# Gated linear attention and SwiGLU: scores and state product moved into 32-column groups of the array, causal mask by predicated copy

## The chip, the cores and the metric

The kernel runs on one core of one Trainium2 chip. The metric is device time in microseconds (us) of one execution. TensorE is called PE in the profile, its weight loads PEld, VectorE is DVE, ScalarE is ACT, GpSimd is POOL and SyncE, which here only issues DMAs, is SP.

## The reference

Two blocks follow each other, everything in fp32. The first is a recurrence for each of 4 batches and 8 heads over 768 positions, with head size 48 and one complex decay per position and feature:

```python
for t in range(S):
    ar, ai = (a_re_n[:, :, t, :, None], a_im_n[:, :, t, :, None])
    new_re = ar * S_re - ai * S_im
    new_im = ar * S_im + ai * S_re
    kv = np.einsum('bhd,bhe->bhde', k[:, :, t], v[:, :, t])
    S_re, S_im = (new_re + kv, new_im)
    y[:, :, t] = np.einsum('bhd,bhde->bhe', q[:, :, t], S_re)
```

`a_re_n` and `a_im_n` are the decay with its magnitude capped at 0.999. The second block takes y as 3072 tokens of 384 features, divides each by its root mean square, scales it, and applies a feed-forward layer of width 1536: `silu(x @ w_gate) * (x @ w_val) @ w_out`.

## The kernel before

**Tiling.** The 768 positions of a batch are cut into chunks of 128 (`C`), which makes 24 chunks. Two chunks form a group of the feed-forward (12 groups), and from the third on also a unit of the decay work. The recurrence becomes matrix products inside a chunk and a state carried from chunk to chunk.

**Stages.** `gates(u)` turns the decays of a unit into cumulative magnitudes and phases on ACT and DVE, multiplies q and k by them (tile `rot`), and moves the result with six DMAs per chunk into `kq`: 96 rows (48 features times cosine and sine part), per head 128 columns of k and 128 of q. `attend(n)` then does for chunk n:

- scores: for each head one product of k (96x128, the stationary operand) with q (96x128, streamed), which gives 128 key positions s by 128 query positions t; four heads fill one PSUM bank (banks 4 and 5, variable `a`). DVE multiplies each bank by a 0/1 matrix `causal` into `am` (line 1080);
- the output, transposed (features by positions): 12 blocks of 32 features, each the sum of `ve` (v, with each pair of heads padded to 80 columns per head so that a block of 32 may be cut anywhere) times `am`, and of the previous state times q. Each block goes to one of four groups of 32 columns of the array, chosen by the 32 PSUM partitions that it writes, and the list is ordered so that the four groups take turns;
- where the batch goes on: k is transposed on PE into `kt` (positions by 96), and the state product adds `kt`^T v for each head: stationary 128x96, streamed 48 columns (line 1112);
- the norm: squares on ACT, a column sum on PE, a power on POOL, and a spread of the result over the partitions on PE, then `xT` on DVE.

`feed(g, xT)` is the feed-forward of a group: 144 fp32 products of 256 columns for `w_gate` and `w_val`, then the output product, from group 2 on as seven products of half size (a Strassen-like scheme that uses the sums of `weight_sums`). An fp32 product appears in the trace as two PE records, one for each pass; the transposes appear as one.

**Order of the work.** Nothing is issued in the order of the source. `Flow` records every operation with an estimated duration and the memory it touches (`note` takes a PSUM bank as a whole), `dates` gives each a due time counted back from its users, and `schedule` picks on every engine the ready operation that is due first. `issue` then emits the instructions in that order, so all of them carry line 648 in the profile and are told apart by their tiles. Each engine runs its own instructions strictly in this order. A changed estimate, or one more operation, can move any other operation on any queue. The feed-forward's due times come from a running sum (`clock`), and attention work is placed between its products.

**Names that the change touches.** `causal`, `ams`, `ves`, `states` (buffers, lines 796 to 830), the fills at the start on POOL (`fill`), `attend` (line 1069), and its estimates passed to `mms`. `moved[n]` are the six moves into `kq` of chunk n, behind which the loads of v are held (`behind=`). SP is the queue for all loads and moves but the weights, which POOL issues.

Of the kernel before, what the change touches and what calls it, by code (L numbers as in the profile page):

```python
# [9 lines left out]
I32 = mybir.dt.int32  # L10
# [4 lines left out]
ALU = mybir.AluOpType  # L15
# [4 lines left out]
C = 128  # L20
BLK = 32
# [440 lines left out]
class Flow:  # L462
# [56 lines left out]
    def add(self, eng, calls, dur, reads=(), writes=(), table=None, land=None, due=None, after=(), behind=()):  # L519
        op = dict(i=len(self.ops), eng=eng, calls=calls, dur=dur, deps=set(), table=table, land=land,  # L520
                  base=due, stage=self.stage, behind={o["i"] for o in behind})
        self.ops.append(op)
        op["deps"].update(o["i"] for o in after)
        for ap in reads:
            self.note(op, ap, False)
        for ap in writes:
            self.note(op, ap, True)
        return op
# [122 lines left out]
def fast(tc, ctx, qT, kT, v, a_re, a_im, w_gate, w_val, w_out, rms_g, out, H, bad):  # L651

    nc = tc.nc
    B, DM, S = a_re.shape
    D = DM // H
    D2 = 2 * D
# [22 lines left out]
    def room(name, shape, dtype=FP32):  # L679
        t = mem.tile(shape, dtype, name=name, tag=name)  # L680
        row = 1
        for x in shape[1:]:
            row *= x
        rooms[t.tensor.name] = (name, row * mybir.dt.size(dtype))
        keep.append(t)
        return t
# [25 lines left out]
    def tt(o, x, y, op=ALU.mult, eng="DVE", **kw):  # L712
        e = nc.vector if eng == "DVE" else nc.gpsimd
        dur = 0.15 + 1.04e-3 * cols(o) if eng == "DVE" else 0.25 + 2.2e-3 * cols(o)
        return add(eng, [(e.tensor_tensor, (), dict(out=o, in0=x, in1=y, op=op))], dur, [x, y], [o], **kw)
# [51 lines left out]
    def dma(o, x, eng="SP", **kw):  # L767
        n = mybir.dt.size(o.dtype)
        for s in o.shape:
            n *= s  # L770
        row = mybir.dt.size(o.dtype) * min(run(o), run(x))
        load = n / row * (0.006 + 50.3e-6 * row) / 16
        op = add(eng, [(QUEUE[eng].dma_start, (), dict(out=o, in_=x))], 0.85 if eng == "POOL" else 0.62, [x], [o],
                 land=2.0 + 1.4 * load, **kw)
        op["load"] = load
        op["packet"] = max(0.07, 0.006 + 50.3e-6 * row * (2 if eng == "POOL" and row == 2048 else 1))
        return op

    def mms(list_, dur, **kw):
        calls, reads, writes = [], [], []  # L780
        for o, l, r, start, stop in list_:
            calls.append((nc.tensor.matmul, (o,), dict(lhsT=l, rhs=r, start=start, stop=stop)))
            reads += [l, r]
            writes.append(o)
        return add("PE", calls, dur, reads, writes, **kw)

    def mm_time(n, m=P):
        return 2 * max(0.84e-3 * n, 0.83e-3 * m)
# [4 lines left out]


    ident = room("ident", [P, P])
    causal = room("causal", [C, C])
    mhalf = room("mhalf", [P, 1])
    ones = room("ones", [P, 1])
    halfpi = room("halfpi", [P, 1])
# [24 lines left out]
    ams = [room(f"am{i}", [C, H, C]) for i in range(2)]  # L824
    kts = [room(f"kt{i}", [C, H, D2]) for i in range(1)]
    ves = [room(f"ve{i}", [C, NP, 2, 80]) for i in range(3)]
    states = [room(f"state{i}", [D2, NP, 2, 80]) for i in range(2)]
    sqs = [room(f"sq{i}", [P, ND, C]) for i in range(1)]
    ygs = [room(f"yg{i}", [P, ND, C]) for i in range(2)]
# [16 lines left out]
    for t in ves + states:  # L846
        fill(t[:, :, :, D:], 0.0)
    add("POOL", [(make_identity, (nc, ident), {})], 0.6, [], [ident])
    fill(causal, 1.0)
    add("POOL", [(nc.gpsimd.affine_select, (), dict(out=causal, in_=causal, pattern=[[1, C]],  # L850
                                                    compare_op=ALU.is_ge, fill=0.0, base=0,
                                                    channel_multiplier=-1))], 0.3, [causal], [causal])
    dma(gcol, rms_g.rearrange("(c p) -> p c", p=P))


# [213 lines left out]
    def attend(n):  # L1069
        flow.stage = "attend", n  # L1070
        ve, am, kq = ves[n % 3], ams[n % 2], kqs[n % 2]
        vv = ve[:, :, :, 0:D].rearrange("t m e d -> t (m e) d")
        dma(vv, v[n * C:(n + 1) * C, :].rearrange("t (h d) -> t h d", d=D), behind=moved[min(n - 1, HOLD)] if n else ())
        k, q = kq[:, :, 0:C], kq[:, :, C:2 * C]
        for a in range(2):
            ps = banks[4 + a]
            s = ps.rearrange("s (h t) -> s h t", h=HH)
            mms([(s[:, h], k[:, a * HH + h], q[:, a * HH + h], True, True) for h in range(HH)],
                HH * mm_time(C), due=EARLY.get(n))
            tt(am[:, a * HH:(a + 1) * HH], s, causal.unsqueeze(1).to_broadcast([C, HH, C]))  # L1080
        first, last = n % NCH == 0, n % NCH == NCH - 1
        prev, new = states[(n + 1) % 2], states[n % 2]
        ps = banks[6]
        yT = ps[:, 0:DM].rearrange("p (j t) -> p j t", j=ND)
        lines = [[] for _ in range(4)]
        vf, sf = (x.rearrange("p m e d -> p m (e d)") for x in (ve, prev))
        for i in range(4 * ND):
            j, c = divmod(i, 4)
            m, r = divmod(i, 3)
            o = yT[c * BLK:(c + 1) * BLK, j]  # L1090
            part = [(2 * m, 0)] if r == 0 else [(2 * m, 1), (2 * m + 1, 2)] if r == 1 else [(2 * m + 1, 3)]
            todo = []
            for h, g in part:
                todo.append((vf[:, m, g * BLK:(g + 1) * BLK], am[:, h]))
                if not first:
                    todo.append((sf[:, m, g * BLK:(g + 1) * BLK], q[:, h]))
            for x, (l_, r_) in enumerate(todo):
                lines[c].append((o, l_, r_, x == 0, x == len(todo) - 1))
        order = [lines[c][i] for i in range(len(lines[0])) for c in range(4)]
        mms(order, len(order) * mm_time(C) / 4 * 1.1 + 0.15)  # L1100
        if not last:
            kt = kts[0]
            for a in range(2):
                ps = banks[7 - 3 * a]
                kp = ps[:, 0:HH * D2].rearrange("t (h d) -> t h d", h=HH)
                calls = [(nc.tensor.transpose, (kp[:, h], k[:, a * HH + h], ident[0:D2, 0:D2]), {})
                         for h in range(HH)]
                add("PE", calls, HH * 0.085, [k[:, a * HH:(a + 1) * HH], ident], [kp])
                act(kt[:, a * HH:(a + 1) * HH], kp, AF.Copy)
            ps = banks[5][0:D2, 0:DM]  # L1110
            st = ps.rearrange("p (h d) -> p h d", h=H)
            mms([(st[:, h], kt[:, h], vv[:, h], True, True) for h in range(H)], H * mm_time(D, D2))
            st4 = ps.rearrange("p (m e d) -> p m e d", m=NP, e=2)
            u, i = unit_of[n], n - UNITS[unit_of[n]][0]
            decay = decays[way_of(u)][:, :, i].rearrange("p (m e) -> p m e", e=2).unsqueeze(3).to_broadcast([D2, NP, 2, D])
            new4 = new[:, :, :, 0:D]
            if first:
                tt(new4, st4, decay)
            else:
                tt(new4, st4, prev[:, :, :, 0:D], ALU.add)  # L1120
                tt(new4, new4, decay)

        flow.stage = "norm", n
        sq, yg = sqs[0], ygs[n % 2]
        act(sq, yT, AF.Square)
        if unit_of[n] in LIGHT:
            for j in range(ND):
                act(yg[:, j], yT[:, j], AF.Copy, scale=gcol[:, j:j + 1])
        else:
            tt(yg, yT, gcol.unsqueeze(2).to_broadcast([P, ND, C]))  # L1130
            tt(sq[:, 0], sq[:, 0], sq[:, 1], ALU.add)
            tt(sq[:, 0], sq[:, 0], sq[:, 2], ALU.add)
        ps = banks[7]
        col = ps[:, C:C + 1]
        parts = range(ND if unit_of[n] in LIGHT else 1)
        mms([(col, sq[:, j], ones, j == 0, j == parts[-1]) for j in parts], 0.25 * len(parts))
        sv = ssv[:, n:n + 1]
        ts(sv, col, 1.0 / DM, EPS_RMS, ALU.mult, ALU.add)
        add("POOL", [(nc.gpsimd.tensor_tensor, (), dict(out=rss[n % 2], in0=sv, in1=mhalf,
                                                        op=ALU.pow))], 0.9, [sv, mhalf], [rss[n % 2]])  # L1140
        wide = ps[:, 0:C]
        mms([(wide, rss[n % 2].to_broadcast([P, P]), ident, True, True)], 0.25)
        g = group_of[n]
        ns = GROUPS[g]
        x, lo = xplace[g]
        wide_ = len(ns) * C
        xT = xTs[x][:, lo:lo + ND * wide_].rearrange("p (j t) -> p j t", j=ND)
        i = n - ns[0]
        tt(xT[:, :, i * C:(i + 1) * C], yg, wide.unsqueeze(1).to_broadcast([P, ND, C]))
        return xT  # L1150
# [190 lines left out]
```

## Time and profile before

| | us |
|---|---|
| median of 3 runs | 740.79 (740.71 to 741.93) |
| profiled execution, its own time | 740.29 |
| its span, first to last instruction | 738.6 |
| PE busy in the span | 694.7 (94%) |
| PEld busy | 623.9 (84%) |
| DVE busy | 470.6 (64%) |
| ACT busy | 332.1 (45%) |
| POOL busy | 39.4 (5%) |
| first product of the feed-forward starts at | 55.41 |

The table is read from the top: the span is what the instructions explain, and the profiled execution's own time is 1.7 us longer. Busy shares are averages over a start in which PE waits for the first decays and weights, and a long stretch in which it hardly waits at all. PE's busy time is the union of its records; the records overlap because the array is pipelined, so how long a product holds the array is read from the distance between the starts of records, not from their durations.

### The profile page before, as it was taken

The page shows a single profiled execution, that of the slowest core. Times are in us where ns is not written, and L with a number is a line of the kernel's source. Part 1 is how long each engine was busy: PE and PEld are TensorE (multiplying, and loading weights), DVE is VectorE, ACT ScalarE, POOL GpSimd, SP SyncE. Part 2 cuts the span into 40 slices and gives each one's busy share as a digit, 9 for nine tenths or more (in the row PEclk, how much of TensorE's full clock was granted, in tenths as well). Part 3 has the DMA queues.
Part 4 walks back from the last instruction along what each step waited for, and adds up shares of the span by engine and source line. Part 5 has one row for each costly group of instructions (what it writes and reads, how often), then busy time and mean ns, then how long its engine had stood idle before and what let it go on. Part 6 is the DMA issues. An engine that isn't in the chain of part 4 may idle for free.

```text
span 738.6 us, 12320 instructions
## 1 busy us (share of the span) xinstructions
PE 694.7 (94%) x5050; PEld 623.9 (84%) x5050; DVE 470.6 (64%) x738; ACT 332.1 (45%) x450; POOL 39.4 (5%) x71
## 2 busy tenths in 40 slices
PE   0369999999999999999999999999999999999996
PEld 0368877877899899899899899899899899899885
DVE  5989987779987977967646546656834234233121
ACT  8567656937576925813915623722821110110010
POOL 3132100000000000000000000000000000000000
PEclk9968999999999999999999999999999999999999
DMA  8697565536455355535222202314111102200000
GB/s 298 209 294 235 161 154 166 163 82 169 127 138 149 99 154 150 181 106 146 70 65 66 75 12 73 95 27 119 54 40 30 51 12 55 65 1 2 22 0 27
DMA packets 100144, 76.47 MB, mean 104 GB/s; under 512 B 40944, under 2 KB 90864, under 8 KB 100080
## 3 DMA queue, kind: packets, MB, share of 16 engines
q1 hardware_dynamic: 96016, 61.05, 30.3%
q0 software_dynamic: 3264, 14.16, 5.3%
q8 instruction: 42, 0.69, 0.4%
q10 hardware_dynamic: 800, 0.39, 0.2%
q14 instruction: 22, 0.18, 0.1%
HBM read 51.91 MB, written 4.72 MB: 77 GB/s over the span
## 4 chain that ended last, share of the span: by engine, by line
PE 92%; DVE 4%; ACT 1%; POOL 1%; issue 1%; DMA 1%; DVEq 0%; POOLq 0%; ACTq 0%
PE bank L648 92%; DVE wg L648 1%; DVE turns L648 1%; DVE wv L648 1%; DMA in<-in_a_re_dram 1%; ACT t L648 0%; DVE t L648 0%; DVE rot L648 0%; ACT L648 0%; DVE in L648 0%; POOL rs L648 0%; DVE xT L648 0%; ACT turns L648 0%; DVE am L648 0%; ACT wo L648 0%
## 5 line engine op out<-in xcount | busy, mean ns | idle before, releaser
L648 PE MATMUL bank<-xT,wg 128*128 128x256 f32 x864 | 201.0, 383 | 1.9 <-DVE xT L648 1.9
L648 PE MATMUL bank<-xT,wv 128*128 128x256 f32 x864 | 198.4, 379 | 0.0
L648 PEld LDWEIGHTS bank<-xT,wg 128*128 128x128 f32 x864 | 164.8, 192 | 25.1 <-DVE xT L648 2.6
L648 PEld LDWEIGHTS bank<-xT,wv 128*128 128x128 f32 x864 | 163.5, 190 | 22.2
L648 DVE TENSOR_TENSOR hT<-bank,sg 128x512 f32<-128x512 f32 x72 | 49.6, 689 | 120.9 <-PE bank L648 114.9
L648 PE MATMUL bank<-wo,hT 128*128 128x192 f32 (+1 forms) x576 | 123.4, 357 | 0.4 <-DVE hT L648 0.4
L648 PEld LDWEIGHTS bank<-wo,hT 128*128 128x128 f32 x576 | 94.4, 190 | 11.8 <-issue 1.4
L648 ACT ACTIVATE sg<-bank 128x512 f32<-128x512 f32 x72 | 43.0, 597 | 130.4 <-PE bank L648 127.4
L648 ACT ACT_TABLE_LOAD x67 | 86.0, 1283 | 7.3 <-DVE rot L648 4.7
L648 PE MATMUL bank<-kq 96*128 96x128 f32 x384 | 52.3, 290 | 28.2 <-DMA kq<-rot 28.2
L648 PEld LDWEIGHTS bank<-kq 96*128 96x128 f32 x384 | 49.5, 203 | 29.8 <-issue 29.0
L648 ACT ACTIVATE sq<-bank 128x384 f32<-128x384 f32 x24 | 11.8, 491 | 106.7 <-PE bank L648 106.6
L648 DVE TENSOR_TENSOR rot<-kin,turns 128x768 f32<-128x768 f32 x48 | 44.6, 952 | 14.6 <-DMA kq<-rot 14.4
L648 POOL TENSOR_TENSOR rs<-ssv,mhalf 128x1 f32<-128x1 f32 x24 | 19.4, 810 | 586.6 <-DVE ssv L648 498.0
L648 ACT ACTIVATE kt<-bank 128x384 f32<-128x384 f32 x40 | 18.5, 489 | 66.0 <-PE bank L648 65.9
L648 PE MATMUL bank<-sums,hT 128*128 128x192 f32 x240 | 45.1, 329 | 0.0
L648 PEld LDWEIGHTS bank<-sums,hT 128*128 128x128 f32 x240 | 39.4, 190 | 0.0
L648 DVE TENSOR_TENSOR hT<-hT 128x768 f32<-128x768 f32 x40 | 38.2, 955 | 0.9
L648 PE MATMUL bank<-am,ve 128*32 128x128 f32 x768 | 37.8, 281 | 0.0
L648 ACT ACTIVATE turns<-in 128x768 f32<-128x768 f32 (+1 forms) x39 | 29.9, 789 | 17.1 <-DVE rot L648 8.0
L648 DVE TENSOR_TENSOR am<-bank,causal 128x512 f32<-128x512 f32 x48 | 32.7, 686 | 7.1 <-PE bank L648 6.5
L648 ACT ACTIVATE t<-t 128x768 f32<-128x768 f32 (+1 forms) x39 | 30.9, 792 | 7.9 <-DVE t L648 7.2
(108 smaller groups left out, 729.0 us busy)
## 6 DMA issues: line engine op xcount, KB each, us to landing
kq<-rot SPq DMA_DIRECT2D x144, 128.0 KB, 2.4
ve<-in_v_dram SPq DMA_DIRECT2D x24, 192.0 KB, 3.1
kin<-in_q_dram SPq DMA_DIRECT2D x24, 192.0 KB, 2.7
kin<-in_k_dram SPq DMA_DIRECT2D x24, 192.0 KB, 4.1
wo<-in_w_gate_dram SPq DMA_DIRECT2D x6, 768.0 KB, 5.7
out_dram<-ot SPq DMA_DIRECT2D x24, 192.0 KB, 2.2
wo<-in_w_val_dram SPq DMA_DIRECT2D x6, 768.0 KB, 4.3
wo<-in_w_out_dram SPq DMA_DIRECT2D x6, 768.0 KB, 4.3
```

The lines of the kernel that those rows point to most:

```text
L648: fn(*args, **kw)
```

## The change

- **Scores.** Instead of one product of 128 stationary columns per head, there are four per head, each with one block of 32 key positions as the stationary operand. Block b streams only the query positions from 32b on (128, 96, 64 and 32 columns); what lies left of it is masked anyway. Block b of an even head is written to partitions 32b to 32b+31, that of an odd head to block 3-b, so that two heads together give every column group 160 columns. The estimate becomes 0.29 per pair of heads.
- **Mask.** Because part of each bank is not written, the product with `causal` becomes a predicated copy: `am` is zeroed once at the start, and only positions where the mask is set are copied from PSUM. The mask has two forms, natural and with its four row blocks reversed; `causal` doubles and is made by eight selects. Banks 4 and 5 are zeroed once on DVE.
- **v.** The odd heads' `am` has its row blocks reversed, so `ve` must hold v of the odd heads with row blocks reversed: one DMA for the even heads and four for the odd ones. The state product needs the natural order, so v is read a second time, whole rows, into the new single buffer `vn`.
- **State product.** The 96 stationary columns of a head are cut into three groups of 32: 24 products per chunk instead of 8, each streaming 48 columns. The estimate becomes 0.1 per head.

```diff
-    causal = room("causal", [C, C])
+    causal = room("causal", [C, 2, C])
...
+    vns = [room(f"vn{i}", [C, H, D]) for i in range(1)]
...
     fill(causal, 1.0)
-    add("POOL", [(nc.gpsimd.affine_select, (), dict(out=causal, in_=causal, pattern=[[1, C]],
-                                                    compare_op=ALU.is_ge, fill=0.0, base=0,
-                                                    channel_multiplier=-1))], 0.3, [causal], [causal])
+    for e in range(2):
+        for b in range(4):
+            x = causal[b * BLK:(b + 1) * BLK, e]
+            add("POOL", [(nc.gpsimd.affine_select, (), dict(out=x, in_=x, pattern=[[1, C]],
+                                                            compare_op=ALU.is_ge, fill=0.0,
+                                                            base=-BLK * (3 - b if e else b),
+                                                            channel_multiplier=-1))], 0.3, [x], [x])
+    for t in ams:
+        fill(t, 0.0)
+    for t in banks[4:6]:
+        fill(t, 0.0, eng="DVE")
...
-        vv = ve[:, :, :, 0:D].rearrange("t m e d -> t (m e) d")
-        dma(vv, v[n * C:(n + 1) * C, :].rearrange("t (h d) -> t h d", d=D), behind=moved[min(n - 1, HOLD)] if n else ())
+        first, last = n % NCH == 0, n % NCH == NCH - 1
+        vv = vns[0]
+        later = dict(behind=moved[min(n - 1, HOLD)] if n else ())
+        rows = v[n * C:(n + 1) * C, :].rearrange("t (m e d) -> t m e d", e=2, d=D)
+        dma(ve[:, :, 0, 0:D], rows[:, :, 0], **later)
+        for b in range(4):
+            dma(ve[(3 - b) * BLK:(4 - b) * BLK, :, 1, 0:D], rows[b * BLK:(b + 1) * BLK, :, 1], **later)
+        if not last:
+            dma(vv.rearrange("t h d -> t (h d)"), v[n * C:(n + 1) * C, :], **later)
...
-            mms([(s[:, h], k[:, a * HH + h], q[:, a * HH + h], True, True) for h in range(HH)],
-                HH * mm_time(C), due=EARLY.get(n))
-            tt(am[:, a * HH:(a + 1) * HH], s, causal.unsqueeze(1).to_broadcast([C, HH, C]))
-        first, last = n % NCH == 0, n % NCH == NCH - 1
+            list_ = []
+            for h in range(HH):
+                for b in range(4):
+                    c = 3 - b if h % 2 else b
+                    list_.append((s[c * BLK:(c + 1) * BLK, h, b * BLK:], k[:, a * HH + h, b * BLK:(b + 1) * BLK],
+                                  q[:, a * HH + h, b * BLK:], True, True))
+            mms(list_, HH // 2 * 0.29, due=EARLY.get(n))
+            pairs = lambda t: t.rearrange("s (m e) t -> s m e t", e=2)
+            mask = causal.bitcast(I32).unsqueeze(1).to_broadcast([C, HH // 2, 2, C])
+            o = am[:, a * HH:(a + 1) * HH]
+            add("DVE", [(nc.vector.copy_predicated, (), dict(out=pairs(o), mask=mask, data=pairs(s)))],
+                0.15 + 1.04e-3 * HH * C, [causal, s, o], [o])
...
-            mms([(st[:, h], kt[:, h], vv[:, h], True, True) for h in range(H)], H * mm_time(D, D2))
+            mms([(st[c * BLK:(c + 1) * BLK, h], kt[:, h, c * BLK:(c + 1) * BLK], vv[:, h], True, True)
+                 for h in range(H) for c in range(3)], H * 0.1)
```

In the order of instructions that results, the pieces of attention lie elsewhere between the feed-forward's products, and the start is arranged anew on every queue. PE enters 32-column products in 53 separate stretches after the first product of the feed-forward, against 23 before (22 of them the output of a chunk, and one product for the final check). After that point there are 22 chunks of scores and 18 state products.

## Prediction

> **What bounds the kernel now.** I first read the chain that ended last, in order of time (start us, us, what):
>
> ```profile
> 55.41 58.15 PE bank L648 x386
> ...
> 116.60 0.46 DVE xT L648
> ...
> 117.10 567.96 PE bank L648 x4226
> ...
> 686.15 40.45 PE bank L648 x200
> ```
>
> From 55.41 to the end at 738.6 the chain is PE's own queue but for some 12 us. The stage table (length, busy time and records of each engine, clock, DMA share) says that the others have room there:
>
> ```profile
> 117.10:686.10 569.00, 568.16 (x4228) 515.44 (x4228) 360.91 (x581) 249.98 (x327) 14.43 (x20) 1.00 0.32 88
> ```
>
> PE is busy for 568.2 of 569.0 us, DVE for 361, DMA for 0.32. So what counts is the array time of the touched products, read from starts in PE's timeline (start, us, instruction):
>
> ```profile
> 317.30 1.48 PE L648 MATMUL bank<-ve,kt 128*96 128x48 f32 x16
> 318.62 1.12 PE L648 MATMUL bank<-kq 96*128 96x128 f32 x8
> 319.58 2.75 PE L648 MATMUL bank<-xT,wv 128*128 128x256 f32 x12
> 322.17 1.06 PE L648 MATMUL bank<-kq 96*128 96x128 f32 x8
> 323.07 0.82 PE L648 MATMUL bank<-ident,kq 96*128 96x96 f32 x8
> ```
>
> A state product holds PE for 318.62-317.30 = 1.32 us (16 records of 0.083), half the scores for 323.07-322.17 = 0.90 (8 of 0.112). Then a stretch in 32-column groups, the output of a chunk:
>
> ```profile
> 337.05 1.14 PE L648 MATMUL bank<-sums,hT 128*128 128x192 f32 x6
> 338.12 0.42 PE L648 MATMUL bank<-am,ve 128*32 128x128 f32 x8
> 338.36 0.40 PE L648 MATMUL bank<-kq,state 96*32 96x128 f32 x8
> 338.58 0.40 PE L648 MATMUL bank<-am,ve 128*32 128x128 f32 x8
> ...
> 339.68 0.40 PE L648 MATMUL bank<-kq,state 96*32 96x128 f32 x8
> 340.01 1.24 PE L648 MATMUL bank<-hT 128*128 128x192 f32 x6
> 341.09 0.38 PE L648 MATMUL bank<-ident,rs 128*128 128x128 f32 x2
> ...
> 342.29 1.14 PE L648 MATMUL bank<-sums,hT 128*128 128x192 f32 x6
> 343.26 0.28 PE L648 MATMUL bank<-ones,sq 128*128 128x1 f32 x2
> ```
>
> Eight records take 0.22 us (338.58-338.36), 0.0275 each, a quarter of the 0.110 that one group needs for 128 columns. But the stretch also costs something at its edges. Six plain products take 343.26-342.29 = 0.97; before the stretch they take 338.12-337.05 = 1.07, after it 341.09-340.01 = 1.08, and its 64 records take 340.01-338.12 = 1.89 where 8 x 0.22 = 1.76 would do. Entering and leaving costs 0.10 + 0.13 + 0.11 = 0.34 us.
>
> Do the groups really run apart? Counts of PE records in flight at another stretch's start:
>
> ```profile
> 329.12:329.16 0.04, 0.02 (x4) 1.00 0.00 0
> 329.16:329.26 0.10, 0.10 (x4) 1.00 0.00 0
> 329.26:329.30 0.04, 0.04 (x8) 1.00 0.00 0
> ```
>
> Four records start within 0.04 us, none in the next 0.10, then four more: each group works through its own two passes.
>
> **What the Trainium skill says.** "TensorEngine Tiling (Array Packing)", Key Properties: tiles load weights and multiply in parallel, and "Changing tiling mode (not just tile) drains the TensorE". The trace agrees with both; its 0.34 us is the drain with the weights reloaded behind it. "TensorE: Matmul & The Clock Gate", Part 1, gives a floor of about 25 ns between starts however small the product; the trace's starts inside a group of four are closer, but its lasting rate, 0.0275, is no proof against such a floor. "VectorE: DVE Perf Modes", perf-mode tier table, has fp32 `tensor_tensor` with a PSUM operand at one element per cycle, which the 0.686 us of the mask's 128x512 product fits; a predicated copy is in neither.
>
> **The change part by part**, after 55.41 (22 chunks of scores, 18 state products).
>
> Removed on PE: 22 x 1.80 + 18 x 1.32 = 39.6 + 23.8 = 63.4 us.
>
> Added: a streamed column costs (0.216-0.1625)/64 = 0.84 ns, from the 0.216 and 0.1625 us of the 256- and 192-column records; 128 columns make 0.107, so 0.110 leaves 0.003 per record. A column group gets 160 columns per pair of heads and pass, in two records: 2 x (160 x 0.00084 + 0.006) = 0.28, for four pairs 1.12 us. The state product gives each of three groups 16 records of 48 columns: 16 x (0.040 + 0.003) = 0.69. Together 22 x 1.12 + 18 x 0.69 = 37.0. Gross gain 26.4 us.
>
> Edges: many new stretches touch one another or an output stretch, so there are 53, 30 more than before: 30 x 0.34 = 10.2. **Net on PE: 16.2 us less.**
>
> Unknown in this is the rate with short records, which no row shows. Below: no better than the columns alone, 1.07 and 0.64, another 2 us. Above: weight loads or issue in one line at 0.0275 per record, treated as the second rival. I take 0.28 per pair because of the counts above.
>
> Mask: the nearest row is the product, 48 x 0.686 on DVE. I take the same. It can hardly be under 0.53 (512 columns at the slope of DVE's fp32 rows, (0.955-0.689)/256 = 1.04 ns each), and at two cycles each it would be 1.2. In the long stretch this is hidden: the 40 copies there would add 20 us to 361 of 569, and the new order leaves at least 2.6 us of PE work between scores and output. Were that cover gone, PE would lose up to 0.5 per copy. At the start, where DVE is the bound, four copies would cost 2 us.
>
> v: 140 loads instead of 24. An issue holds SP for 0.60 us, so 116 more make 70 us, some 3 per chunk; the extra bytes, 20 x 192 KB = 3.9 MB of 76, are hidden by DMA's 0.32. Behind them on SP wait the six `kq` moves, and behind those the scores; `vn` is one buffer, so its load also holds SP until the last state product is through. SP waits 165 us for PE as it is, so I cost this at nothing; uncovered, each load delays the scores by 0.6.
>
> Start: POOL's wide fill and seven more selects (about 1.0 and 7 x 0.25 us by the 128x256 fill and the one select) push the first weight load from 4.0 to some 5.5; DVE's two bank fills lie before its first input at 5.65. The weights are converted only after chunk 0's rotation in the new order, which covers the delay. On DVE the chunk-0 rotation ends about 0.9 earlier, and its later work is the same sum with fewer waits: walked through with the old durations, the second `xT` could come at 52.8 instead of 55.35. Against it, ACT squares unit 2's decays ahead of chunk 1's squares, and those decays landed at 46.0 to 48.1 and now stand behind three more loads, so about 54. I take 1 us gained, between 3 gained and 2 lost.
>
> Sum: 738.6-16.2-1.0 = 721.4 span. The profiled time is 1.7 above its span, the median 0.5 above that: **723.5 us**.
>
> **Rivals.** *New waits.* PE gets ahead of the queues. In the trace the `kq` of one chunk landed at 215.2 and its scores began at 215.8, so such a margin can be eaten by v loads ahead of the moves. If ten pairs of chunks lose 1 us each: 733.5; case range 729 to 741. Against it: the order is planned with these loads in it.
>
> *Slower: records, not columns, set the pace.* If weight loads of different groups, or the issue, come one after another at 0.0275 per record, scores cost 64 x 0.0275 = 1.76 and the state product 48 x 0.0275 = 1.32: gross gain 0.9, edges 10.2, total 749. At the skill's 25 ns (an estimate from that page): 56.8 against 63.4, total 743. It decides from (63.4-10.2)/2272 records = 23.4 ns on; I expect 16.3. For it: every lasting rate in the trace is 0.0275 or more. Against it: the counts, and that PE queues instructions ahead during long products.
>
> *Better:* edges cheaper in short stretches and the full 3 us at the start: 712 to 718.
>
> **How the numbers follow.** As worked out 0.68 (own range 718 to 729); new waits 0.13, of which 0.02 ends within 0.2% of before and 0.01 above; slower 0.14; better 0.05. A difference of 0.2% is about what a measurement of this kernel can tell from none. Faster 0.68+0.10+0.05 = 0.83, same 0.02, slower 0.15. The range 717 to 741 leaves out the slower case and most of the better one.
>
> **What would show it.** In PE's timeline: 32 score records in about 0.56 us and 48 state records in 0.69 between starts; about 0.34 lost per stretch; PE gapless from about 54. If 32 score records take 0.8 or more, the second rival is right; if PE idles for `kq`, `ve` or `am`, the first. A predicated copy well over 0.7 us would make the start wrong. The forecast fails most easily at the rate of short records.

## The result, and the profile after

The changed kernel takes 735.44 us (median of 5 runs, 733.58 to 737.05) against 740.79 (5 runs, 740.57 to 741.93): a ratio of 0.9925, 95% interval 0.9906 to 0.9944. That is 5.4 us faster, where 17.3 were forecast. The profiled execution took 735.44 us, with a span of 733.7.

The chain that ended last, in order of time (start us, us, what), has PE's own queue in it as before, but in shorter pieces:

```profile
237.87 97.36 PE bank L648 x905
...
351.18 329.02 PE bank L648 x3042
...
681.30 40.45 PE bank L648 x200
```

Before, one piece ran from 117.10 to 685. Now pieces end at 335 and begin again at 351, with turns of SP's queue, a landing of `kq` and VectorE's `rot` and `xT` in between (the chain runs through them; PE itself stands still there for 0.98 us). The waits of PE after its first feed-forward product (who waits <- for whom: us in total, times, longest) show the same. First the kernel before, from 55 us on:

```profile
PE bank L648 <- DVE xT L648: 1.9, 3, 0.9
PE bank L648 <- DVE hT L648: 0.4, 1, 0.4
```

Then the changed kernel, from 58 us on:

```profile
PE bank L648 <- DVE xT L648: 2.8, 4, 1.0
PE bank L648 <- DVE am L648: 2.0, 1, 2.0
PE bank L648 <- ACT kt L648: 1.6, 1, 1.6
PE bank L648 <- DMA kq<-rot: 0.8, 1, 0.8
PE bank L648 <- DVE hT L648: 0.4, 1, 0.4
```

Three new kinds of wait have come: for the mask (`am`), for the transposed keys (`kt`) and for the moves into `kq`. The products themselves are nearly as short as hoped. PE's timeline (start, us, instruction) around a state product and half of a chunk's scores:

```profile
321.85 0.88 PE L648 MATMUL bank<-vn,kt 128*32 128x48 f32 x48
322.64 0.77 PE L648 MATMUL bank<-kq 96*32 96x128 f32 x32
323.34 2.86 PE L648 MATMUL bank<-xT,wv 128*128 128x256 f32 x12
```

From start to start, 48 state records take 322.64 - 321.85 = 0.79 us and 32 score records 323.34 - 322.64 = 0.70, edges included. The forecast was 0.69 and 0.56 without edges.

Now add up where the time after the first feed-forward product went, from starts in PE's timeline by kind of product (us, before then after): scores 40.2 to 30.1, state product 23.9 to 16.5, output of the chunks 39.1 to 39.5, transposes 12.7 to 14.6, feed-forward 533.7 to 538.9, column sums and spreads 9.9 to 11.7. A wait of PE is inside the stretch that it follows. (The 144 products of `w_gate` and `w_val` in a group, as the kernel before was described, are 144 records in the trace, two for each of 72 products.) The sum, up to the product for the final check, falls from 659.6 to 651.5; the 17.2 us of products behind that one are the same in both. The gaps of PE behind the first feed-forward product (those over 0.04 us) grow from 1.6 to 8.1. (Of the 2.3 us in the list of waits before, 0.7 lies ahead of that product.) So PE's own work fell by 8.1 + 6.4 = 14.5. And the first feed-forward product starts at 58.65 instead of 55.41.

The forecast span was 721.4, the measured one is 733.7. The 12.3 us between them are: start 58.65 instead of the 54.4 in the forecast, 4.25; new gaps, 6.4; PE's own work, 16.2 forecast and 14.5 found, 1.7. So the array did roughly what was promised, and over 10 of the 12 us went elsewhere. The experiments ask why.

### The profile page after: what moved, and what is told of

Same layout as the page of the kernel before. It is cut to its first block, busy times and chain, and to the rows that moved or that the text cites. A ratio compares the mean times of both kernels' runs of the same rounds, so it can differ in the third digit from the quotient of the medians.

```text
span 733.7 us, 16076 instructions
## 1 busy us (share of the span) xinstructions
PE 679.7 (93%) x6842; PEld 598.6 (82%) x6842; DVE 473.2 (64%) x740; ACT 331.3 (45%) x451; POOL 42.0 (6%) x80
## 2 busy tenths in 40 slices
DMA packets 104575, 80.64 MB, mean 110 GB/s; under 512 B 42800, under 2 KB 95280, under 8 KB 104496
## 4 chain that ended last, share of the span: by engine, by line
PE 64%; DVE 2%; DMA 2%; SPq 2%; ACT 1%; issue 0%; DVEq 0%; ACTq 0%
PE bank L648 64%; SPq L648 2%; DMA kq<-rot 1%; DMA in<-in_a_im_dram 1%; DVE turns L648 0%; DVE t L648 0%; ACT turns L648 0%; DVE hT L648 0%; DVE large L648 0%; DVE xT L648 0%; DVE in L648 0%; ACT L648 0%; DVE small L648 0%; DVE ot L648 0%; DVE rot L648 0%
## 5 line engine op out<-in xcount | busy, mean ns | idle before, releaser
L648 PE MATMUL bank<-kq 96*32 96x96 f32 (+3 forms) x1536 | 35.5, 243 | 33.8 <-DVE wg L648 28.2
L648 PEld LDWEIGHTS bank<-kq 96*32 96x32 f32 x1536 | 31.7, 114 | 39.7 <-DVE wg L648 28.2
L648 ACT ACTIVATE sq<-bank 128x384 f32<-128x384 f32 x24 | 11.7, 487 | 96.5 <-PE bank L648 95.8
L648 PE MATMUL bank<-am,ve 128*32 128x128 f32 x768 | 41.4, 290 | 0.4 <-DMA ve<-in_v_dram 0.4
L648 DVE COPY_PREDICATED am<-causal,bank 128x512 f32<-128x512 int32 x48 | 32.9, 720 | 8.1 <-PE bank L648 8.1
L648 PE MATMUL bank<-kq,state 96*32 96x128 f32 x640 | 35.6, 285 | 0.0
```

What stands on the lines that cost most here:

```text
L648: fn(*args, **kw)
```

## Theories

- **A, the v loads.** 140 loads instead of 24 take turns on SP ahead of the moves into `kq` and of the next decays.
- **B, the plan.** The new estimates and operations made the planner put all other work in another order, and that order is worse, with or without the loads.
- **E, the setup.** Eight selects and the first of the two fills of `am` stand on GpSimd ahead of the first weight load, which is issued at 6.09 us instead of 4.02.
- **D, the packed work itself.** Once PE is faster, other engines are late in any order.

## Are the loads to blame?

**One load, the changed kernel's order.** The plan is made with six loads, then five are emptied:

```diff
+        for x in loads[1:]:
+            x["calls"] = []
+        loads[0]["calls"] = [(nc.sync.dma_start, (), dict(out=vh, in_=...))]   # all heads, natural order
...
-            mms([(st[...], kt[...], vv[:, h], True, True) ...
+            # the same products, reading vh
```

> The changed kernel with its order of work kept, but one v load per chunk in place of six: v lands in natural order, and the state product reads that tile. The odd heads' rows of v then don't match their block-reversed scores, so that part of the output isn't the reference's; every product, record and mask is the same size as in the changed kernel. Theory A (the lost time comes from the v loads: their turns in SP's queue ahead of the key and query moves and of the input loads): the first feed-forward product starts by 55.5 us, TensorE's gaps after it fall from 8.0 us to about 3, and the time is 726 to 729 us. Theory B (it comes from the new order in which the planner put the other work): first product near 58.6, gaps of 7 to 8 us stay, and the time is 734 to 736 us.

Measured: 733.28 us (731.37 to 733.79), ratio 0.9887 (0.9874 to 0.9901). That is 2.2 us below the changed kernel, not 6 to 9. The first feed-forward product came at 60.80 and the gaps were 6.1 us. As a theory of the whole loss, A falls.

**The loads alone.** The kernel before, with five loads into `ve` (natural order) and one into `vn`:

```diff
-        dma(vv, v[n * C:(n + 1) * C, :].rearrange("t (h d) -> t h d", d=D), ...)
+        dma(ve[:, :, 0, 0:D], rows[:, :, 0], **later)
+        for b in range(4):
+            dma(ve[b * BLK:(b + 1) * BLK, :, 1, 0:D], rows[b * BLK:(b + 1) * BLK, :, 1], **later)
+        if n % NCH != NCH - 1:
+            dma(vv.rearrange("t h d -> t (h d)"), v[n * C:(n + 1) * C, :], **later)
```

> The kernel before (scores, mask and state product untouched) with the changed kernel's six v loads per chunk, in natural order, and the state product reading the second copy. Theory A: the loads cost 6 to 9 us by themselves, 746 to 750 us, with a later first feed-forward product (58 to 59) and new gaps behind the key and query moves. Theory B: 740 to 742 us, like the kernel before.

Measured: 743.08 (742.56 to 744.11), ratio 1.0031 (1.002 to 1.0043), first product at 55.75. The loads cost 2.1 us here too. Neither theory had that number.

**The loads on GpSimd's queue.**

```diff
-            dma(ve[(3 - b) * BLK:(4 - b) * BLK, :, 1, 0:D], rows[...], **later)
+            dma(ve[(3 - b) * BLK:(4 - b) * BLK, :, 1, 0:D], rows[...], "POOL", **later)
...
-            dma(vv.rearrange("t h d -> t (h d)"), v[...], **later)
+            dma(vv.rearrange("t h d -> t (h d)"), v[...], "POOL", **later)
```

> The changed kernel whose four odd-head v loads and second copy of v go through GpSimd's queue; only the even heads' load stays in SP's. The bytes and packets are the same. Theory A in its form 'SP's turns are what is late': first product by 56, gaps under 4 us, 726 to 730 us. Theory A in its form 'the packets are in the way on the DMA engines': 733 us or more with the key and query moves landing as late as in the changed kernel. Theory B: 734 to 737 us.

Measured: 736.65 (735.55 to 739.49), ratio 0.9951 (0.9935 to 0.9967). The stretch after PE's first product, up to the final check, was the shortest of these (645.5 us with 4.4 of gaps), but that product came at 64.96. The plan had changed again: ScalarE waited until 53.88 for a piece of the weights and then did unit 2's decays ahead of chunk 1's squares, which start at 59.18. The v loads now also share GpSimd's queue with the weights, and the two causes aren't parted. Nor does this run tell SP's turns from the packets; it was the first hint at B.

## Is it the plan?

**State product alone.** The kernel before, with one edit: no further loads, no fills, no predicated copy.

```diff
-            mms([(st[:, h], kt[:, h], vv[:, h], True, True) for h in range(H)], H * mm_time(D, D2))
+            mms([(st[c * BLK:(c + 1) * BLK, h], kt[:, h, c * BLK:(c + 1) * BLK], vv[:, h], True, True)
+                 for h in range(H) for c in range(3)], H * 0.1)
```

> The kernel before with the state product alone in three column groups. It reads the one v tile, so that there is no further load. By the prediction's terms: 18 products at 0.69 for 1.32 us take 11.3 us away, 16 more 32-column stretches at 0.34 us bring 5.4 back: 740.8 - 5.9 = 735 us (733 to 737), with gaps as in the kernel before. If the planner's changed estimates alone bring waits (theory B), 738 us or more, with gaps over 5 us.

Measured: 738.66 (736.88 to 739.99), ratio 0.9969 (0.9958 to 0.998). After the first feed-forward product PE takes 6.7 us less, gaps included, more than the 5.9 of the sum. But that product starts at 59.50, 4.1 later. So the time is the one that B asked for, but by a late start and not by gaps over 5 us (2.8 were found). In the start nothing was touched but two state products and the place of instructions. What moved is seen on ScalarE. Before, chunk 1's squares (`sq`) go ahead of unit 2's decays:

```profile
48.94 0.52 ACT L648 ACTIVATE sq<-bank 128x384 f32<-128x384 f32 x1
...
50.49 0.86 ACT L648 ACTIVATE t<-in 128x768 f32<-128x768 f32 x1
51.35 1.28 ACT L648 ACT_TABLE_LOAD   x1
```

In the changed kernel the decays go first, wait for their load, and bring a change of the activation table with them:

```profile
50.27 0.84 ACT L648 ACTIVATE t<-in 128x768 f32<-128x768 f32 x1 [2.58 <-DMA in<-in_a_re_dram]
51.12 1.28 ACT L648 ACT_TABLE_LOAD   x1
52.41 0.84 ACT L648 ACTIVATE turns<-in 128x768 f32<-128x768 f32 x1
53.16 0.47 ACT L648 ACTIVATE sq<-bank 128x384 f32<-128x384 f32 x1
```

The squares start 4.2 us later, and chunk 1's norm and the feed-forward hang on them. The run with the state product alone has the same order there (squares at 54.10); what the decays stand behind in it is a piece of the weights, for which ScalarE waits until 49.65.

**Prices alone.** The kernel before, with the two durations that the planner is given:

```diff
-                HH * mm_time(C), due=EARLY.get(n))
+                HH // 2 * 0.29, due=EARLY.get(n))
...
-            mms([...], H * mm_time(D, D2))
+            mms([...], H * 0.1)
```

> The kernel before with nothing changed but the two durations that the planner is given for the scores (1.16 for the old estimate) and the state product (1.6), as the changed kernel gives them. Only the order of instructions moves. Theory B: the first feed-forward product at 58 to 60 us and more gaps, 743 to 747 us. Theory D: 740 to 742 us.

Measured: 741.15 (739.37 to 745.23), ratio 1.0015 (1.0002 to 1.0028). The first product came at 57.03, 1.6 later, but the rest was nearly as good as before (gaps of 2.6 us for 1.6). So these prices don't make every plan worse; this run went as D had it.

**The changed kernel with the old prices**, the reverse edit:

```diff
-            mms(list_, HH // 2 * 0.29, due=EARLY.get(n))
+            mms(list_, HH * mm_time(C), due=EARLY.get(n))
...
-                 for h in range(H) for c in range(3)], H * 0.1)
+                 for h in range(H) for c in range(3)], H * mm_time(D, D2))
```

> The changed kernel with the planner's old durations for scores and state product; the six loads, the fills and the second copy of v are planned as in the changed kernel. If the two durations alone set off the new order, 727 to 731 us with a first feed-forward product by 57; if any new operation reshuffles the plan, 732 to 738 us with a first product at 58 or later.

Measured: 733.13 (729.8 to 735.8), ratio 0.9906 (0.9881 to 0.9931), 2.3 us below the changed kernel, with few gaps (4.4 us) and a late first product (60.31). That is the second answer: the two durations alone don't set off the new order.

**All the packed work in the old order, one load.** The planner makes the plan of the kernel before; only then are the instructions of its scores, masks, state products and setup exchanged:

```diff
             op = mms([(s[:, h], k[:, a * HH + h], q[:, a * HH + h], True, True) for h in range(HH)], ...)
+            op["calls"] = [...]        # the 16 packed products of the half
             op = tt(am[:, a * HH:(a + 1) * HH], s, causal[:, 0]...)
+            op["calls"] = [(nc.vector.copy_predicated, ...)]
...
             op = mms([(st[:, h], kt[:, h], vv[:, h], True, True) for h in range(H)], ...)
+            op["calls"] = [...]        # the 24 packed products
```

> All of the packed work (scores, state product, predicated copies, the causal table and the fills) put in place of the old instructions after the planner has made the old kernel's plan, so that every engine keeps the order of the kernel before; v comes with the old single load, so that the odd heads' rows of v are in natural order against block-reversed scores, and that part of the output isn't the reference's. Theory B (the planner's new order lost the time): first feed-forward product at 55 to 57 us, gaps after it under 4 us, TensorE 26.4 less and 33 more 32-column stretches at 0.34 (11.2) more: 740.9 - 15.2 = 725 to 728 us. Theory D (the packed work itself leaves other engines late, whatever the order): 732 us or more, with gaps of 6 us and over.

Measured: 730.98 (728.75 to 731.62), ratio 0.9862 (0.9846 to 0.9878): 4.5 us below the changed kernel, 3 to 6 above what B asked and 1 below what D asked. First product 58.05, gaps 4.1. The run to compare it with is the one with one load in the changed kernel's order: it is 2.3 us below that, and the two intervals (0.9846 to 0.9878, 0.9874 to 0.9901) just touch. The old order is somewhat better for the packed work, but not free of waits.

**The old order with six loads.** As the last, but with v in both orders: the five loads of `ve` stand where the one stood, and a copy of the odd heads goes into one of two buffers `vn`, its load behind the state product that frees it.

```diff
+        put += [(ve[(3 - b) * BLK:(4 - b) * BLK, :, 1, 0:D], rows[...]) for b in range(4)]
+        load["calls"] = [(nc.sync.dma_start, (), dict(out=o_, in_=x_)) for o_, x_ in put]
+        vload[n] = [(nc.sync.dma_start, (), dict(out=vn, in_=rows[:, :, 1]))] if not last else []
+        (sts[n - 2] if n - 2 in sts else load)["calls"] += vload[n]
```

> As the run with the old order, but with v in two orders: five loads into the attention tile and one of the odd heads alone (half the bytes of the changed kernel's second copy) into two buffers; the state product takes even heads from the first and odd heads from the second. Each load stands where the old one stood, the odd heads' second copy after the state product that frees its buffer. Theory B: 2 to 3 us over the run with one load, 727 to 731 us, below both kernels. Theory D: 734 us or more.

Measured: 750.76 (746.42 to 752.17), ratio 1.013 (1.0108 to 1.0152), 20 us above the run with one load. B's number misses. D's "734 or more" is met, but not for D's reason: the packed work and the order are those of the run with one load. Its span is 19.2 us longer: 5.0 by the start (63.02), 9.9 by gaps (14.0 in all) and 4.4 by PE's own work, where PE's granted clock falls to half behind three of the gaps. Its chain of waits shows the way a load becomes a gap:

```profile
352.80 0.61 SPq L648
...
353.45 2.40 DMA kq<-rot
...
356.85 0.56 DVE xT L648
```

A turn of SP, the move into `kq` behind it, VectorE's `rot` that waits for that move, and `xT` queued behind `rot`: PE stands still for 3.83 us until 357.45. SP's own timeline shows what the move stood behind:

```profile
338.37 4.57 SPq L648 DMA_DIRECT2D kq<-rot  x6
342.98 3.23 SPq L648 DMA_DIRECT2D ve<-in_v_dram  x5
346.25 0.61 SPq L648 DMA_DIRECT2D vn<-in_v_dram  x1
346.90 5.21 SPq L648 DMA_DIRECT2D decay<-ends  x6
352.21 3.77 SPq L648 DMA_DIRECT2D kq<-rot  x6
```

SP has no break here, and the six loads take 3.8 us of its turns. A gap of 2.3 us at 528 has the same chain; one of 3.6 at 295 ends on a landing of `w_out` instead. So the forecast's "0.6 us per load, uncovered" is real. In the changed kernel the planner had made room for the loads; its new order isn't only a loss.

## Is it the setup?

**Setup and mask alone**, in the order of the kernel before:

```diff
+    edge["calls"].append((nc.gpsimd.affine_select, ...))                     # eight instead of one
+    edge["calls"] += [(nc.gpsimd.memset, (t, 0.0), {}) for t in ams]
+    edge["calls"] += [(nc.vector.memset, (t, 0.0), {}) for t in banks[4:6]]
...
             op = tt(am[:, a * HH:(a + 1) * HH], s, causal[:, 0]...)
+            op["calls"] = [(nc.vector.copy_predicated, ...)]
```

> The kernel before, its order kept, with the changed kernel's setup and mask alone: eight selects for the causal table in place of one, the two fills of the masked scores and the two of the banks, and predicated copies in place of the multiplications by the mask; scores, state product and v as before. Theory E (the setup on GpSimd stands ahead of the first weight loads and delays the start): the first weight load is issued some 3 to 4 us later, the first feed-forward product comes at 57.5 to 58.5 us, and the time is 742.5 to 744 us. Rival (the start has slack, and the predicated copy costs nothing): 740 to 741.5 us.

Measured: 742.18 (740.89 to 743.29), ratio 1.0015 (1.0008 to 1.0023), first product 56.81, 1.4 later. That lies between the two answers: setup and mask have a part, of 1.3 us. Here the first weight load is issued at 8.02, later than in the changed kernel, because both fills of `am` stand ahead of it. The copies, at 0.72 us against the product's 0.686, add no more than is in this number.

**Setup late.** In the changed kernel the selects and fills are held behind the second weight load:

```diff
-    fill(causal, 1.0)
+    fill(causal, 1.0, behind=[posted[1]])      # and likewise the selects and the fills of am
```

> The changed kernel with the causal table's selects and the fills of the masked scores held behind the issue of the second weight load on GpSimd, where it waits for a landing anyway. Theory E: the first weight load is back at 4.0 us, the first product at 56 to 57, the time 732.5 to 734 us. Rival (what delays the start is ScalarE's place for the next unit's gate work, or the v loads): 735 to 736 us.

Measured: 728.69 (727.31 to 728.95), ratio 0.9832 (0.9819 to 0.9844): 6.7 us below the changed kernel and 12 below the kernel before. That is far more than E's price. Two companions on the same chip warn against reading it as E: with the old prices added (the edit shown above under that name),

> As the run with the planner's old durations, with the setup held behind the second weight load as well. Theory E: 2 us under the run with old durations alone (733.1), 730.5 to 732 us. Rival: 732.5 to 734 us.

it is 733.60 (731.33 to 734.72), ratio 0.9899 (0.9883 to 0.9914), no lower than the run with the old prices and early setup (733.13). The two kernels with late setup issue the same instructions; they differ in two numbers given to the planner, and by 4.9 us. And with, on top of that, the second copy of v for odd heads only, in two buffers,

```diff
-    vns = [room(f"vn{i}", [C, H, D]) for i in range(1)]
+    vns = [room(f"vn{i}", [C, NP, D]) for i in range(2)]
...
-            dma(vv.rearrange("t h d -> t (h d)"), v[n * C:(n + 1) * C, :], **later)
+            dma(vv, rows[:, :, 1], **later)
```

> As the run with old durations and late setup, and the second copy of v holds the odd heads alone, in two buffers; the state product takes even heads from the attention tile. The same number of loads, half the bytes of the second copy, and no wait of a load on the state product of the chunk before. If waits of SP's queue on the single second buffer cost time: 728 to 730 us, below every kernel so far. If not: within 1 us of the run with late setup and old durations.

it is 739.50 (737.19 to 744.94), ratio 0.9988 (0.9972 to 1.0004), outside both answers, with the first product at 64.12. It moves 2 MB less in all (78.7 for 80.6), but in 112,255 packets instead of 104,575, since whole rows of v are no longer read in one piece. Whether the packets or the plan made the start late isn't separated.

## Plan and setup crossed

To part the two, each of the two plans was run with the setup early and late, with no other instruction moved. (The second fill of `am` is late in all four, as it is in the changed kernel.) Late setup in the changed kernel's plan:

```diff
     flow.schedule()
+    for x in setup:
+        posted[1]["calls"] = posted[1]["calls"] + x["calls"]
+        x["calls"] = []
```

> The changed kernel's own plan on every engine; only the setup's instructions on GpSimd (causal table, fills of the masked scores) are issued after the second weight load in place of before the first. If the run with late setup won its 6.7 us by the earlier weight loads themselves: 728.5 to 730.5 us, first feed-forward product at 56 to 57. If it won them by the new plan that came with it, beyond some 2 us: 732.5 to 735 us, with the gaps of the changed kernel (98 to 102, 125, 238, 351 us) in their places.

Measured: 733.85 (730.0 to 735.17), ratio 0.9904 (0.9882 to 0.9925), with gaps of 1.1 and 1.8 us at 97 and 101 us again. Early setup in the plan of the run with late setup, by the same means (`lead` is a fill at the head of GpSimd's queue):

```diff
     flow.schedule()
+    for x in setup[:-1]:
+        lead["calls"] = lead["calls"] + x["calls"]
+        x["calls"] = []
```

> The reverse: the plan of the run with late setup on every engine, but the causal table and the first fill of the masked scores issued at the head of GpSimd's queue, ahead of the first weight load. If the earlier loads won the time: 733.5 to 736 us. If the plan won it: 729.5 to 731.5 us, with the first product 1 to 2.5 us later than in the run with late setup.

Measured: 728.29 (727.44 to 728.61), ratio 0.9831 (0.9818 to 0.9844).

| median us | setup early | setup late |
|---|---|---|
| the changed kernel's plan | 735.44 | 733.85 |
| the plan of the run with late setup | 728.29 | 728.69 |

By the ratios to the kernel before the rows are 0.9925 and 0.9904, then 0.9831 and 0.9832. The plan is worth 5.2 to 7.2 us. The setup's place is worth nothing in the lower plan; the 1.6 in the upper one can't be told from nothing, since the intervals (0.9906 to 0.9944, 0.9882 to 0.9925) overlap. PE's waits in the run at the lower left, from 57 us on:

```profile
PE bank L648 <- DVE xT L648: 3.0, 5, 0.9
PE bank L648 <- DVE hT L648: 0.4, 1, 0.4
```

The waits for `am`, `kt` and `kq` are gone, though all six loads, the selects and the packed products are there. Its span is 7.1 us shorter than the changed kernel's: 1.0 by the start (57.66), 5.3 by gaps (2.8 in all) and 0.9 by PE's own work, though one state product more (0.8) lies behind its first feed-forward product.

**The loads in the good plan.** One load, by the first experiment's edit on the run with late setup:

> The plan of the run with late setup, with one v load per chunk in natural order and the other five left out; the odd heads' rows of v don't match their block-reversed scores, so that part of the output isn't the reference's. It prices the five further loads where the plan is good. If they cost what they did in the changed kernel's plan (735.4 against 733.3): 726 to 727.5 us. If the plan hides them: 728 to 729.5 us.

Measured: 726.91 (724.58 to 727.77), ratio 0.9807 (0.979 to 0.9823): 1.8 us, with an interval that overlaps a little with that of the run with six loads. The loads cost about 2 us in either plan.

**One place in the plan.** The longest gap of the changed kernel is at 99.8 us. VectorE's timeline there:

```profile
97.69 1.84 DVE L648 SCALAR_TENSOR_TENSOR wo<-hT,wo 128x768 int32<-128x768 int32 x2
...
100.20 0.94 DVE L648 CUSTOM_DVE_ANT_0 wo<-hT,wo 128x1536 uint16<-128x1536 uint16 x1
101.07 1.32 DVE L648 COPY_PREDICATED am<-causal,bank 128x512 f32<-128x512 int32 x2
```

Conversion passes of the weights stand ahead of chunk 2's two copies. In the better plan (the run with early setup) the copies stand first:

```profile
95.57 1.34 DVE L648 COPY_PREDICATED am<-causal,bank 128x512 f32<-128x512 int32 x2 [1.53 <-PE bank L648]
96.82 1.79 DVE L648 SCALAR_TENSOR_TENSOR wo<-hT,wo 128x768 int32<-128x768 int32 x2
```

What the gap brings after it is seen in the stage table (length, busy time and records of PE, PEld, DVE, ACT, POOL, then PE's granted clock, DMA share, GB/s):

```profile
101.83:104.00 2.17, 2.17 (x48) 2.04 (x52) 2.17 (x4) 0.49 (x1) 0.00 (x0) 0.76 1.13 229
104.00:106.00 2.00, 2.00 (x59) 1.99 (x54) 2.00 (x2) 0.53 (x2) 0.00 (x0) 0.50 0.21 21
106.00:108.00 2.00, 2.00 (x66) 1.85 (x59) 1.08 (x3) 1.97 (x5) 0.29 (x1) 0.91 0.21 34
```

PE works again but at half clock for a while: 0.24 x 2.17 + 0.50 x 2 + 0.09 x 2 = 1.7 us more. That is as much as PE's own work differs between the two plans when the same products are counted (0.9 and the 0.8 of the state product). Moving one conversion pass of each of the two pieces behind the copies, and nothing else:

```diff
     flow.schedule()
+    for i, t in ((199, 0.1), (194, 0.2)):       # one pass each of the last two w_out pieces
+        flow.ops[i]["order"] = flow.ops[360]["order"] + t
```

> The changed kernel with two instructions moved in VectorE's queue and nothing else: at about 98 to 101 us, one conversion pass of each of the last two w_out pieces is issued after chunk 2's two predicated copies in place of before them. The 2.0 us gap of TensorE at 99.8 us should shrink to about 0.5 to 1, and the half-speed clock at 102.5 to 107 us (1.7 us) should not come. If those two are a piece of the loss: 731.5 to 733 us. If the gap only moves on to the next user of the weights or of the copies: 734.5 to 736 us.

Measured: 734.43 (732.2 to 739.34), ratio 0.9918 (0.9893 to 0.9943). The profiled execution (732.2) lost both the gap and the half clock behind it, but PE then stood still 1.4 us later in the same chunk:

```profile
103.46 0.92 PE L648 MATMUL bank<-vn,kt 128*32 128x48 f32 x48 [1.36 <-ACT kt L648]
```

The median is 1 us below the changed kernel's, with runs that overlap, so that it isn't shown that this place costs the kernel anything by itself; in the profiled execution part of its gap moved on to the next user. This one exchange, the only one tried, doesn't give the 5 to 7 us. In the traces the 5.3 us of gaps lie at several places, the longest at 98 to 102, 238 and 351 us.

## Why the prediction was right or wrong

The step that failed is the order of the work: the sum took the planner's new order as free of new waits, because it "is planned with these loads in it", and as 1 us better at the start. Measured were 6.4 us of new gaps and a start 3.2 us later, together 10.7 of the 12.3 us that the span missed. The term of the array, which the text called the one most easily wrong, held. Term by term:

- **Net on PE, 16.2 us less.** Nearly right: 14.5 in the changed kernel. The 1.7 that are missing are as much as the half clock costs, which the sum had no term for. In the run with early setup in the better plan, without a long gap, it is 15.4 with one state product more, so 16.2 for the same products. That this agrees to a tenth is luck: at the start the clock is at half as well, for 4.75 us behind the first feed-forward product before, 3.33 in the changed kernel and 4.45 in that run, which shifts these numbers by up to 0.7.
- **Short records.** Right: 32 score records cost 0.70 with their edges and 48 state records 0.79, which refutes the rival in which records set the pace at 0.0275 each (0.88 and 1.32 before any edge). A record of the state product takes 16.5 ns or less (0.79/48, edges included), below the 25 ns that the Trainium skill, "TensorE: Matmul & The Clock Gate", Part 1, has as the least distance of starts; with three column groups at work the measurement decides.
- **Edges.** The trace after has the first feed-forward product behind a 32-column stretch longer by 0.104 us (0.320 for 0.216), as before, and 53 stretches. That part held.
- **v loads "costed at nothing".** Wrong by 2 us: 2.2, 2.1 and 1.8 in three pairs of runs. The reason given, SP's slack of 165 us, was the wrong measure: a sum of waiting says nothing about the turns that stand between a `rot` and its moves. The text named that danger and its price of 0.6 each; the run with the old order, which wasn't planned with six loads, is 20 us slower for them.
- **"The order is planned with these loads in it."** This stood against the rival of new waits, and was the largest miss. Gaps are what came (6.4 us, chance 0.13 given). But their cause was not mainly the loads, which the rival named: it was the order as a whole, worth 5.2 to 7.2 us with the setup and all six loads in place. The planner's estimates are no guarantee, and with identical instructions two of its plans differ by 4.9 us. That the rival's 733.5 lies near the measured 735.4 is in part luck: it counted ten pairs of chunks at 1 us each and no loss at the start.
- **Start, 1 us gained.** Wrong in sign: 3.2 lost. The walk along VectorE took every other queue as it was planned. The text had seen that ScalarE squares unit 2's decays ahead of chunk 1's squares, but counted the landing of those decays (put at about 54, seen at 50.2 for the first), not the 1.28 us table change and the second pass that come with it. In the better plan the squares stand ahead of the decays again (51.94 us in the run with early setup, 53.16 in the changed kernel). Setup and mask cost 1.3 in the order of the kernel before, but the setup's place costs nothing in the better plan, so what it has in the 3.2 stays open. In no run with packed products did the first feed-forward product come before 56.1 us, with one load or six, setup early or late: the start is not PE's to shorten. What holds the better plans at 57 was not taken apart.
- **Mask at nothing.** Held within what was measured: 0.72 us per copy, and 1.3 us for mask and setup together. The wait of 2.0 us for `am` comes from the place of two copies in VectorE's queue, not from their length.

For the run with late setup the same terms are smaller: 721.4 + 2.55 (start 56.96 for 54.4) + 2.45 (gaps 4.1 for 1.6) + 0.6 (15.6 on PE for 16.2) = 727.0, its span. So even in this plan 5.6 us of the forecast are missing, 2.55 of them at the start.

## What to carry to other kernels

Where a planner orders the queues, a change has two effects: the instructions and the new order. Price the first from the rows, but give the second a range of its own, here 5 to 7 us of 740 between two plans of one kernel, and make more than one plan before judging the change: the same instructions in another order gave 728.7 instead of 735.4. Part the two by exchanging instructions after the plan is made. And count a wait of PE with what follows it, since its clock may fall to half behind the gap.

## What was not expected of the hardware

After a gap of 2.0 us, with another of 0.8 shortly before it, PE's granted clock fell to 0.50 for 3.4 us, from 1.1 us after work had resumed; in the gap itself it showed 1.00. A gap of 1.65 us at 236 us, alone, had no such effect, nor had one of 1.93 in the run with the old prices. The run with the old order and six loads has three such stretches, one of them behind a single gap of 2.28 us (PE's timeline, then the stage table as above):

```profile
528.17 4.02 PE L648 MATMUL bank<-xT,wg 128*128 128x256 f32 x10 [2.28 <-DVE xT L648]
528.02:531.43 3.41, 3.26 (x8) 2.63 (x9) 3.30 (x7) 0.73 (x1) 0.00 (x0) 0.50 0.46 91
```

Each of these stretches lasts 3.41 us and so costs 1.7. The Trainium skill, "TensorE: Matmul & The Clock Gate", Part 1, has the half rate after an idle window of about 3.4 us; the traces agree on the half, while 2.3 us of idle time in one piece, or 2.8 within 4.6, were enough here. Gaps of 1.1 and 1.6 us within 4.5, in the changed kernel with one load, were not, so the sum of idle time doesn't settle it; what does isn't shown here.

The rows of single heads (192 bytes) cost more packets than the whole rows that they are part of: half the bytes of the second copy made 7,680 packets more (112,255 for 104,575). What the packets cost in time isn't shown.
